# Chunked attention and a gated feed-forward layer on one core: memory values spread in pieces, 1e-9 added by ScalarE, scratch products planned singly, halo rows of two units loaded

## The chip, the cores and the metric

The kernel runs on one core of a Trainium2 chip. The metric is the device time of one execution in microseconds (us). Before the change the median of three runs is 397.0 us (395.86, 397.0, 401.0). The profiled execution, from which all durations below come, took 398.16 us.

## What is computed

Four batches, eight heads, 768 positions, head size 64; the attention looks at a chunk of 32 queries with 16 keys to its left, 8 to its right, and 8 memory keys. Its output, with the heads joined to 512 columns, goes through a gated feed-forward layer.

```python
for c in range(nc):                                   # 24 chunks of 32 queries
    k_ctx, v_ctx = k[:, :, l_start:r_end], v[:, :, l_start:r_end]     # 16 left, 32, 8 right
    k_full = np.concatenate([mem_k, k_ctx], axis=2); v_full = np.concatenate([mem_v, v_ctx], axis=2)
    scores = scale * np.matmul(q_c, k_full.transpose(0, 1, 3, 2))
    a = np.exp(scores - np.max(scores, axis=-1, keepdims=True))
    out[:, :, c_start:c_end] = np.matmul(a / (np.sum(a, axis=-1, keepdims=True) + 1e-09), v_full)
h = np.maximum(x @ w_in, 0.0)                         # x: the attention's output, 512 -> 1024
u, v = h[..., :512], h[..., 512:]
v_n = (v - mean(v)) / np.sqrt(var(v) + 1e-06)
v_s = np.einsum('ts,bsd->btd', w_spatial, v_n) + b_spatial[None, :, None]
return (u * v_s) @ w_out
```

## The kernel before

**Units.** The work on attention is cut into 24 units of 128 queries (four chunks; six units to a batch). For a unit TensorE (PE) makes the scores in a burst of 32 small matmuls (`burst`, line 546, tile `sx`), VectorE (DVE) takes the maximum and subtracts it (lines 635, 639), ScalarE (ACT) takes the exponential (line 654), PE turns the result round with four transposes (line 682, tile `pt`), ACT copies it to `pT` (line 685), and PE multiplies it with the values in a second burst of 32 (line 546, tile `f` for the first three units, `sx` later). DVE scales the product with one over the row sum (`norm`, lines 604 and 609), PE turns it round (line 699, tile `xt`), and ACT and DVE split it into a high and a low part (lines 705 and 709), the input `x` of the feed-forward layer. Here s0, p0 stand for the score burst and the value burst of unit 0, and so on.

**Row sums.** For the first three units (`PSUMS = 3`) PE makes the sums itself: four matmuls of `pT` with a tile of two columns, `halves`, ahead of the value burst; `recip` (lines 620, 622) adds 1e-9 and takes the reciprocal. For later units `den` does it on DVE: a reduction (line 659), the addition of a tile `tiny` that holds 1e-9 (line 660), the reciprocal (line 662).

**Values.** For a chunk, 32 partitions hold its own 32 rows of v, 24 more the halo (the next rows), and the last 8 the memory rows. `vmain` holds three units, `v2` three more. The halo of a unit is either loaded (`load_v` with `halo=True`) or copied on the chip from the next chunk's rows (`shift_v`, line 486, by ACT or GpSimd (POOL), two copies for a unit). The memory rows come by small DMAs on ACT's queue (`load_mem`, `mem_rows`); `spread` and `copy_mem` copy them to all the chunks of `vmain` and `v2` (line 316).

**Weights.** `w_in` comes in eight parts, written here w(c, p): c is one of four slices of 128 rows, p=1 the half that makes v, p=0 the half that makes u. The parts arrive as float64 bits, and `from_f64` turns each into a high and a low float32 part: ACT scales two halves (lines 913, 918), DVE shifts and joins the sign (922, 923), POOL adds (928), ACT casts the high part `win_h` (931), POOL subtracts for the low part `win_l` (935). A feed-forward group for one block of 128 tokens (`ffn_v`, `group`) is four pairs, c = 0 to 3, each of three matmuls with N = 512 (lines 748, 749, 750: high times high, low times high, high times low).

**Order.** `Plan` writes the whole program's order: each operation has an engine, a duration from a table, a rank and its dependencies, and a list scheduler places it; the constants at the top (`FIRST`, `HOT`, `AHEAD`, `SPLIT` and so on) steer it. `FIRST` is the order of the first loads, all on SP's queue, as ("w", c, p, rank, ...), ("qk", group, units, pieces), ("v", unit, units, halo). `AHEAD` is the number of bytes that may be under way on that queue before the next load has to wait for an older one. `HOT` says how many scratch matmuls of a tile `minus` with itself (`heat`, line 306, N = 512, into the spare tile `xt`) stand between the first bursts; nobody reads them. `XLOW` is the number of units whose low part is made by PE and ACT (`rest`, `low_copy`) rather than by DVE. Every engine runs its list strictly in order. In the profile, "issue" is time in which an engine waited for nothing that the profile shows.

Of the kernel before, what the change touches and what calls it, by code (L numbers as in the profile page):

```python
# [8 lines left out]
F32 = mybir.dt.float32  # L9
# [9 lines left out]
CH = 32  # L19
# [14 lines left out]
HOT = (7, 4, 3, 7, 7, 0, 0)  # L34
# [12 lines left out]
SPREAD = {"ACT": 2.6, "POOL": 3.0}  # L47
# [29 lines left out]
class Plan:  # L77
# [36 lines left out]
    def order(self):  # L114
# [19 lines left out]
        while len(out) < len(ops):  # L134
# [29 lines left out]
            if count:  # L164
                k, heat = clock.of(t), 0.5 if count in (128, 256) else 1.0
# [39 lines left out]
def tile_chunked_attention_gmlp(  # L205
# [94 lines left out]

    def heat(n, r=()):
        def go():
            if ("xt", "warm") not in t_:
                alloc("xt", "warm", [P, 512], F32, psum=True)
            for _ in range(n):
                nc.tensor.matmul(t_["xt", "warm"], minus, minus.unsqueeze(1).broadcast_to([P, T, P]), start=True, stop=True, skip_group_check=True)  # L306
# [6 lines left out]
    op("DVE", 0.2, clear, w=["clear"], rank=-1.0)  # L313
# [135 lines left out]
    def load_v(i, units=1, halo=True):  # L449
# [4 lines left out]
        last = (i + units) % GU == 0  # L454
        TS = 2 * NC * D
# [34 lines left out]
    def v_keys(i):  # L490
        mem = [("early", 0, "mem", r, *x) for r in range(2) for x in ((), (1,))] if GU <= i < UB else \
# [5 lines left out]

    def copy_mem():
        for r in range(2):
            rows = slice(r * D + CH, (r + 1) * D)  # L500

            def go(e, rows=rows):
                o = v2[rows, :, 0:NV * UC - 1]
                copy_on(e, o, vmain[rows, :, 0:1].broadcast_to(o.shape))
            op(SPREAD, 0, go, r=[("mv", 0, r, 0)], w=[("early", 0, "mem", r)] +
               [("early", j, "v", r, 3) for j in range(GU, UB)], rank=12.0)
            load(v2[(r + 1) * D - M:(r + 1) * D, :, NV * UC - 1], mem_rows(0, r), w=[("early", 0, "mem", r, 1)],
                 rank=12.0, rows=M, us=0.3)

    def load_mem(b, eng="SP", engines=()):  # L510
        for r in range(2):
            rows = vmain[(r + 1) * D - M:(r + 1) * D]
            if not engines:
                for t in range(T):
# [4 lines left out]
            low = vmain[r * D + CH:(r + 1) * D]  # L519

            def spread(e, low=low):
                o = low[:, :, 1:NV * UC - 1]
                copy_on(e, o, low[:, :, 0:1].broadcast_to(o.shape))
            load(rows[:, :, 0], mem_rows(b, r), r=["clear"], w=[("mv", b, r, 0)], rank=10.0 * UB * b, eng=eng, rows=M,
                 us=0.3)
            load(rows[:, :, NV * UC - 1], mem_rows(b, r), w=[("mv", b, r, 2)], rank=10.0 * UB * b, eng=eng, rows=M, us=0.3)
            op(SPREAD, 0, spread, r=[("mv", b, r, 0)], w=[("mv", b, r, 1)] + [("vm", j, r, 3) for j in range(GU)],
               rank=10.0 * UB * b)
# [15 lines left out]
    def burst(i, rank):  # L544
# [5 lines left out]
        for part in ["sp"] if both else ["s", "p"]:  # L550
# [33 lines left out]
            if i >= 1 and "p" in part:  # L584
# [3 lines left out]
                if part == "p" and i - 1 < PSUMS:  # L588
                    us += 0.6
# [470 lines left out]
```

## Time and profile before

| what | value |
|---|---|
| median of three runs | 397.0 us |
| the profiled execution | 398.16 us |
| its span, first to last instruction | 396.1 us |
| instructions | 11126 |
| PE busy / DVE / ACT / POOL | 383.8 / 195.7 / 165.1 / 110.3 us |
| granted PE clock, mean over the span | 0.983 |
| read from and written to memory | 32.52 and 6.29 MB |

The profile has a page with the busy time of each engine and the span in 40 slices, a chain of waits followed back from the last instruction, groups of instructions with their durations, and tables of stretches of time (busy us of each engine, the granted PE clock, the share and rate of the DMA engines). Times are us from the span's start unless marked ns.

### The profile page before, as it was taken

Reading aid. Unit: us, or ns where it says so; the run is one execution under the profiler, and the core shown is the slowest. Engines: PE = TensorE matmul, PEld = TensorE weight load, DVE = VectorE, ACT = ScalarE, POOL = GpSimd, SP = SyncE. Lnnn points to the kernel's source line nnn. Section 1 sums busy time; section 2 is a strip of 40 time slices with the busy share of each in tenths; the row PEclk is TensorE's granted clock in tenths of the full one; section 3 lists DMA queues with packets and bytes.
Section 4 is the critical chain, followed back from the end, with each engine's and each line's share of the span. In section 5 each row is a group of like instructions: output and inputs, shape, how many; then the busy total and the mean of one; then the engine's idle time right before and its main releaser. Section 6 shows DMA issues by size and latency. Waiting matters only on the chain.

```text
span 396.1 us, 11126 instructions
## 1 busy us (share of the span) xinstructions
PE 383.8 (97%) x4864; PEld 344.3 (87%) x4864; DVE 195.7 (49%) x392; ACT 165.1 (42%) x289; POOL 110.3 (28%) x119
## 2 busy tenths in 40 slices
PE   6797999999999999999999999999999999999996
PEld 4586898999899889889988988889989889899995
DVE  2746987895546447494662315383423233514040
ACT  6686986872524235344323223343221223321212
POOL 6497686285102101010220312010222210104031
PEclk9868999999999999999999999999999999999999
DMA  7999337972165582023746010000001010000202
GB/s 249 263 289 300 120 101 159 280 211 76 43 217 79 133 267 73 2 62 121 164 134 233 1 75 7 0 3 2 2 36 46 26 55 0 0 2 0 81 1 79
DMA packets 29216, 39.53 MB, mean 100 GB/s; under 512 B 5360, under 2 KB 23280, under 8 KB 29168
## 3 DMA queue, kind: packets, MB, share of 16 engines
q1 hardware_dynamic: 28864, 38.73, 32.7%
q8 instruction: 38, 0.62, 0.7%
q10 hardware_dynamic: 304, 0.10, 0.1%
q14 instruction: 10, 0.08, 0.1%
HBM read 32.52 MB, written 6.29 MB: 98 GB/s over the span
## 4 chain that ended last, share of the span: by engine, by line
PE 91%; DMA 7%; issue 1%; POOL 1%; SPq 0%; ACT 0%; POOLq 0%
PE f L748 26%; PE f L749 25%; PE f L750 25%; PE sx L546 8%; DMA vmain<-in_v_dram 3%; PE xt L699 3%; PE pt L682 3%; DMA big<-in_moe_w_in_dram 1%; PE f L546 1%; DMA k<-in_k_dram 1%; DMA vmain<-in_mem_v_dram 1%; PE xt L306 1%; POOL vmain L486 1%; SPq L338 0%; ACT st L890 0%
## 5 line engine op out<-in xcount | busy, mean ns | idle before, releaser
L858 POOL TENSOR_TENSOR st<-st,u 128x384 f32<-128x384 f32 x32 | 33.8, 1057 | 139.3 <-DVE st L854 106.0
L748 PE MATMUL f<-wsp_h,vn 128*128 128x384 f32 x192 | 66.4, 346 | 0.0
L749 PE MATMUL f<-wsp_h,vn 128*128 128x384 f32 x192 | 65.0, 339 | 0.0
L750 PE MATMUL f<-wsp_l,vn 128*128 128x384 f32 x192 | 64.5, 336 | 0.0
L786 POOL TENSOR_TENSOR rstd<-ve,mhalf 128x1 f32<-128x1 f32 x24 | 16.6, 691 | 102.2 <-DVE ve L782 102.2
L748 PE MATMUL f<-x,win_h 128*128 128x384 f32 x128 | 44.7, 350 | 0.0
L861 ACT CAST big<-st 128x384 fp32r<-128x384 f32 x32 | 16.4, 512 | 65.1 <-POOL st L858 65.1
L749 PE MATMUL f<-x,win_l 128*128 128x384 f32 x128 | 43.3, 338 | 0.0
L750 PE MATMUL f<-x,win_h 128*128 128x384 f32 x128 | 43.2, 337 | 0.0
L854 DVE TENSOR_TENSOR st<-f,bias 128x384 f32<-128x384 f32 x32 | 17.8, 556 | 51.3 <-PE f L750 51.3
L748 PE MATMUL f<-win_h,x 128*128 128x512 f32 x96 | 39.7, 413 | 0.0
L748 PE MATMUL f<-wout,big 128*128 128x512 f32 (+1 forms) x100 | 39.0, 390 | 0.0
L749 PE MATMUL f<-wout,big 128*128 128x512 f32 (+1 forms) x100 | 38.3, 383 | 0.0
L750 PE MATMUL f<-wout,big 128*128 128x512 f32 (+1 forms) x100 | 38.2, 382 | 0.0
L750 PE MATMUL f<-win_l,x 128*128 128x512 f32 x96 | 38.1, 397 | 0.0
L749 PE MATMUL f<-win_h,x 128*128 128x512 f32 x96 | 38.0, 396 | 0.0
L748 PEld LDWEIGHTS f<-wsp_h,vn 128*128 128x128 f32 x192 | 36.0, 188 | 1.4
L749 PEld LDWEIGHTS f<-wsp_h,vn 128*128 128x128 f32 x192 | 36.1, 188 | 0.8
L750 PEld LDWEIGHTS f<-wsp_l,vn 128*128 128x128 f32 x192 | 36.1, 188 | 0.0
L778 DVE BATCH_NORM_STATS2 stats<-st 128x6 f32<-128x512 f32 x24 | 16.6, 690 | 31.6 <-ACT st L774 31.6
L865 DVE TENSOR_TENSOR big<-st,big 128x384 fp32r<-128x384 f32 x32 | 20.6, 645 | 21.9 <-ACT big L861 21.6
L890 ACT COPY st<-f 128x512 f32<-128x512 f32 (+1 forms) x25 | 14.2, 571 | 31.3 <-PE f L750 30.9
(85 smaller groups left out, 704.8 us busy)
## 6 DMA issues: line engine op xcount, KB each, us to landing
out_dram<-st SPq DMA_DIRECT2D x23, 256.0 KB
k<-in_k_dram SPq DMA_DIRECT2D x7, 800.0 KB
q<-in_q_dram SPq DMA_DIRECT2D x7, 768.0 KB
vmain<-in_v_dram SPq DMA_DIRECT2D x36, 128.0 KB
big<-in_moe_w_in_dram SPq DMA_DIRECT2D x8, 512.0 KB
vmain<-in_v_dram SPq DMA_DIRECT2D x35, 96.0 KB
big<-in_moe_w_spatial_dram SPq DMA_DIRECT2D x6, 384.0 KB
big<-in_moe_w_out_dram SPq DMA_DIRECT2D x4, 512.0 KB
```

What stands on the lines that cost most here:

```text
L546: nc.tensor.matmul(o, w_, m, start=start, stop=True, skip_group_check=True)
L682: nc.tensor.transpose(a[:, t], p[:, t], ident)
L748: nc.tensor.matmul(o, lh, rh, start=(j == 0), stop=False)
L749: nc.tensor.matmul(o, ll, rh, start=False, stop=False)
L750: nc.tensor.matmul(o, lh, rl, start=False, stop=(j == len(pairs) - 1))
L778: nc.vector.bn_stats(stats, t_["st", s])
L786: nc.gpsimd.tensor_tensor(a, t_["ve", i], mhalf, op=ALU.pow)
L854: nc.vector.tensor_tensor(alloc("st", s_, [P, HT], F32), t_["f", n], bias[:, tok], op=ALU.add)
L858: nc.gpsimd.tensor_tensor(a, a, t_["u", i], op=ALU.mult)
L861: nc.scalar.copy(t_["g", i][:, 0, 0:HT], t_["st", s_])
L865: nc.vector.tensor_tensor(a[:, 1, 0:HT], t_["st", s_], a[:, 0, 0:HT].bitcast(F32), op=ALU.subtract)
L890: nc.scalar.copy(alloc("st", s_, [P, N], F32), t_["f", n])
```

## The change

- **Spreading the memory values.** The eight rows of each head half are loaded once, into chunk 0 of `v2` (two DMAs on ACT's queue, not four there and two on SP's). A helper `spread` then copies that chunk to all of `vmain` and to the rest of `v2`, one copy for each of the four head pairs, over all 128 partitions. The copies into `vmain` now also count as writers of all its rows, so v's first loads come after them. The zeroing (`clear`) is one instruction over 128 partitions.
- **1e-9 by ScalarE.** `den` is cut in three: DVE reduces, ACT adds 1e-9 (`plus`), DVE takes the reciprocal (`over`). `PSUMS` is 0, so no unit has its sums made by PE.
- **Scratch products planned singly.** `heat` enters each scratch matmul as an operation of its own; `HOT` is another list, 37 in all and not 28, one of them in a tile of `f` (`heat_f`).
- **Halo rows loaded.** `FIRST` loads units 4 and 5 with their halo, and `shift_v` is left out for them. The order of the first loads is another, q and k come in two pieces, and `AHEAD` is 1.4 MB, not 2.0.
- `XLOW` is 2, `VACT` 4 and not 6 (units whose normalization is on ACT), `VLOW` may use POOL, and the conversion's shift and sign are two planned operations.

```diff
-AHEAD = 2000000
+AHEAD = 1400000
-FIRST = [("qk", 0, (0, 0), 1), ("mem", 0, "ACT", True), ("qk", 0, (1, 2), 2), ("w", 1, 1, 40.0, 3.0),
+FIRST = [("qk", 0, (0, 0), 2), ("mem", 0, "ACT", True), ("w", 2, 0, 35.0, 27.0, 0),
...
-HOT = (7, 4, 3, 7, 7, 0, 0)
+HOT = (4, 9, 2, 12, 6, 0, 3, 1, 0)
-XLOW = 0
-PSUMS = 3
-VACT = 6
+XLOW = 2
+PSUMS = 0
+VACT = 4
-VLOW = {"DVE": 0.85}
+VLOW = {"DVE": 0.85, "POOL": 1.3}
-SPREAD = {"ACT": 2.6, "POOL": 3.0}
+SPREAD = {"ACT": 0.69, "POOL": 0.78}
...
+    def heat_f(n, r):
+        key_ = ("warm", len(plan.ops))
+        def go():
+            a = alloc("f", key_, [P, 512], F32, psum=True)
+            for _ in range(n):
+                nc.tensor.matmul(a, minus, minus.unsqueeze(1).broadcast_to([P, T, P]), start=True, stop=True,
+                                 skip_group_check=True)
+        if n:
+            op("PE", 0.233 * n, go, r=r, w=[("f", key_)], rank=99.0, tail=0.25, count=2 * n)
...
-            for _ in range(n):
+            for _ in range(1):
                 nc.tensor.matmul(t_["xt", "warm"], minus, minus.unsqueeze(1).broadcast_to([P, T, P]), start=True, stop=True, skip_group_check=True)
-        if n:
-            op("PE", 0.233 * n, go, r=r, w=[("xt", "warm")], rank=99.0, tail=0.25, count=2 * n)
+        for _ in range(n):
+            op("PE", 0.233, go, r=r, w=[("xt", "warm")], rank=99.0, tail=-0.03, count=2)
...
-        for r in range(2):
-            nc.vector.memset(vmain[r * D + CH:(r + 1) * D, :, 0], 0.0)
+        nc.vector.memset(v2[:, :, 0], 0.0)
...
+    def spread(name, dst, c0, keys, rank):
+        for t in range(T):
+            def go(e, t=t):
+                o = dst[:, t, c0:NV * UC]
+                copy_on(e, o, v2[:, t, 0:1].broadcast_to(o.shape))
+            op(SPREAD, 0, go, r=["mv0", "mv1"], w=[(name, t)], rank=rank)
+        op("DVE", 0.0, lambda: None, r=[(name, t) for t in range(T)], w=keys, rank=-1.0)
...
+            load(v2[(r + 1) * D - M:(r + 1) * D, :, 0], mem_rows(b, r), r=["clear"], w=[f"mv{r}"], rank=0.0, eng=eng,
+                 rows=M, us=0.3)
+        if engines:
+            spread("spread", vmain, 0, [("mv", b, r, 1) for r in range(2)] +
+                   [("vm", j, r, x) for j in range(GU) for r in range(2) for x in range(4)], 0.0)
...
             nc.vector.tensor_reduce(d, p3, axis=AX.X, op=ALU.add)
-            nc.vector.tensor_tensor(d, d, tiny, op=ALU.add)
+        def plus():
+            nc.scalar.activation(t_["den", i], t_["den", i], AF.Identity, bias=tiny[:, 0:1])
+        def over():
             rec = t_["rec", i] = small.tile([P, T, 2], F32, tag="rec", name="rec")
-            nc.vector.reciprocal(rec.rearrange("p t r -> p (t r)"), d)
+            nc.vector.reciprocal(rec.rearrange("p t r -> p (t r)"), t_["den", i])
...
-            op("DVE", dve(512) + 0.38, den, r=[("p", i)], w=[("rec", i)], rank=rank + 0.6)
+            op("DVE", dve(512) + 0.02, den, r=[("p", i)], w=[("den", i)], rank=rank + 0.6)
+            op("ACT", 0.21, plus, w=[("den", i)], rank=rank + 0.6)
+            op("DVE", 0.23, over, r=[("den", i)], w=[("rec", i)], rank=rank + 0.6)
...
     for i in range(UB):
-        shift_v(i)
+        if i not in whole_v:
+            shift_v(i)
```

**SP's first loads.** On SP's queue, from the start; `big` is a part of w_in, `v_94` is `v2`. Before:

```order
L338 DMA q<-in_q_dram 128x4x128
L338 DMA k<-in_k_dram 128x4x144
L338 DMA q<-in_q_dram 128x2x256 x2
L338 DMA k<-in_k_dram 128x2x256 x2
L338 DMA big<-in_moe_w_in_dram 128x1024 x4
L338 DMA vmain<-in_v_dram 32x4x768 x2
L338 DMA vmain<-in_v_dram 24x4x64 x2
L338 DMA big<-in_moe_w_in_dram 128x1024
L338 DMA q_297<-in_q_dram 128x4x384
L338 DMA k_158<-in_k_dram 128x4x400
L338 DMA v_94<-in_mem_v_dram 8x4x64 x2
L338 DMA big<-in_moe_w_in_dram 128x1024 x2
```

After:

```order
L348 DMA q<-in_q_dram 128x2x128 x2
L348 DMA k<-in_k_dram 128x2x144 x2
L348 DMA big<-in_moe_w_in_dram 128x1024 x2
L348 DMA q<-in_q_dram 128x2x256 x2
L348 DMA k<-in_k_dram 128x2x256 x2
L348 DMA big<-in_moe_w_in_dram 128x1024 x2
L348 DMA vmain<-in_v_dram 32x4x768 x2
L348 DMA vmain<-in_v_dram 24x4x64 x2
L348 DMA q_300<-in_q_dram 128x2x384 x2
L348 DMA k_153<-in_k_dram 128x2x400 x2
L348 DMA big<-in_moe_w_in_dram 128x1024 x4
```

Four parts of w_in still stand ahead of unit 0's values, in both the last bytes of v end about 4.6 MB into the stream. The fifth part, w(2,1), stood right behind them (before: up to 5.2 MB); now the keys of units 3 to 5 and two other parts, w(0,0) and w(3,0), stand ahead of it, so that it ends at 7.7 MB.

**ACT while unit 0's values come in.** ACT's list from the first copies of halo rows on. Before:

```order
L486 COPY vmain<-vmain 24x4x256 x2
L931 CAST win_h<-st 128x512
L654 ACTIVATE p<-p 128x512
L486 COPY vmain<-vmain 24x4x256
L918 ACTIVATE big<-big 128x512
L931 CAST win_h<-st 128x512
L918 ACTIVATE big<-big 128x512
L685 COPY pT<-pt 128x512
L654 ACTIVATE p<-p 128x512
L931 CAST win_h<-st 128x512
L913 ACTIVATE st<-big 128x512
L316 COPY k_158<-k_158 128x16x24
```

After (the first copy of halo rows and the addition of 1e-9 for unit 1 stand ahead of these):

```order
L498 COPY vmain<-vmain 24x4x256
L952 CAST win_h<-st 128x512
L498 COPY vmain<-vmain 24x4x256
L663 ACTIVATE p<-p 128x512
L701 COPY pT<-pt 128x512
L498 COPY vmain<-vmain 24x4x192
L723 CAST x<-xt 128x4x128
L672 ACTIVATE den<-den,tiny 128x8
L326 COPY k_153<-k_153 128x16x24
L701 COPY pT<-pt 128x512
L737 CAST x<-xt 128x4x128
```

ACT has four copies of halo rows here, not three, and the new instructions `den` and the second `x` (unit 0's low part); fewer conversions stand between them. Behind these rows follow: a cast of a weight, both scalings of w(0,0), x of unit 1, the exponential of unit 3, a scaling of w(3,0), both scalings of w(2,1), unit 1's low part, `pT` of unit 3, `den`, a scaling, x of unit 2, a halo copy of unit 3 and then the cast of w(2,1).

**PE's first feed-forward groups.** With the buffers' numbers: one number of `f` is one block of tokens, in each three rows are one pair c. Before, from the first block's third pair on:

```order
L748 MATMUL f_580<-win_h_107,x_475 128x512
L749 MATMUL f_580<-win_h_107,x_475 128x512
L750 MATMUL f_580<-win_l_108,x_475 128x512
L748 MATMUL f_622<-win_h_107,x_475 128x512
L749 MATMUL f_622<-win_h_107,x_475 128x512
L750 MATMUL f_622<-win_l_108,x_475 128x512
```

After, from the second block's second pair on (`f_582` is the first block, `f_630` the second, `f_653` the third):

```order
L766 MATMUL f_630<-win_h_107,x_473 128x512
L767 MATMUL f_630<-win_h_107,x_473 128x512
L768 MATMUL f_630<-win_l_108,x_473 128x512
L766 MATMUL f_653<-win_h_107,x_473 128x512
L767 MATMUL f_653<-win_h_107,x_473 128x512
L768 MATMUL f_653<-win_l_108,x_473 128x512
L553 MATMUL sx_660<-k1_153,q1_300 32x64 x32
L553 MATMUL sx_660<-v2_94,pT_619 32x64 x32
L766 MATMUL f_582<-win_h_107,x_473 128x512
```

Before, the first block runs through c = 0, 1, 2 with one pair of the second block between, and seven pairs stand ahead of the bursts s4 and p3. Now five pairs stand ahead of them, all with c = 0 and 1, from three blocks; the first pair that needs w(2,1) comes behind p3. Just ahead of all this, where before came p0, its transposes, 7 scratch matmuls, the sums and p1 and the rest up to p2, there now stand p0, a scratch matmul, the transposes of unit 0's output, p1, `pt` of unit 2, unit 0's `rest`, s3, p2, the transposes of unit 1's output, and the first pair.

More of the change, by code (lines that the diff above doesn't have):

```diff
@@ L164, in order @@
             if count:
-                k, heat = clock.of(t), 0.5 if count in (128, 256) else 1.0
+                k, heat = clock.of(t), 0.5 if count in (128, 144, 256) else 1.0
                 us *= k if heat == 1.0 else 1.0 if k == 1.0 else 1.36
@@ L454, in load_v @@
         last = (i + units) % GU == 0
+        if halo:
+            whole_v.update(range(i, i + units))
         TS = 2 * NC * D
@@ L490, in v_keys @@
     def v_keys(i):
-        mem = [("early", 0, "mem", r, *x) for r in range(2) for x in ((), (1,))] if GU <= i < UB else \
+        mem = [("early", 0, "mem", r) for r in range(2)] if GU <= i < UB else \
             [("mv", i // UB, r, s) for r in range(2) for s in range(T)]
@@ L496, in mem_rows @@
         return src(mem_v, (b * H + r) * M * D, [[D, M], [2 * M * D, T], [1, D]])
-    def copy_mem():
[L499 to L508, printed above, removed]
+    def spread(name, dst, c0, keys, rank):
[5 more added lines that the diff above has]
+        op("DVE", 0.0, lambda: None, r=[(name, t) for t in range(T)], w=keys, rank=-1.0)
+    def copy_mem():
+        spread("spread2", v2, 1, [("early", 0, "mem", r) for r in range(2)] +
+               [("early", j, "v", r, x) for j in range(GU, UB) for r in range(2) for x in range(4)], 12.0)
     def load_mem(b, eng="SP", engines=()):
         for r in range(2):
-            rows = vmain[(r + 1) * D - M:(r + 1) * D]
             if not engines:
+                rows = vmain[(r + 1) * D - M:(r + 1) * D]
                 for t in range(T):
@@ L517, in load_mem @@
                 continue
[L519 to L528, printed above, removed]
+            load(v2[(r + 1) * D - M:(r + 1) * D, :, 0], mem_rows(b, r), r=["clear"], w=[f"mv{r}"], rank=0.0, eng=eng,
[3 more added lines that the diff above has]
+                   [("vm", j, r, x) for j in range(GU) for r in range(2) for x in range(4)], 0.0)
     def prep(i, rank):
@@ L588, in burst @@
                 if part == "p" and i - 1 < PSUMS:
-                    us += 0.6
+                    us += 1.05
             if i < 3 and len(hot) > 6:
@@ L592, in burst @@
             op("PE", us, go, r=reads, w=writes, rank=rank, tail=0.25, count=128 * len(part) + (16 if us > 1.3 and part == "p" else 0))
+            if (i, part) == (2, "p") and len(hot) > 8:
+                heat_f(hot[8], [("heat", i, part)])
             if i < 3 and len(hot) > 6 and (i, part) != (2, "p"):
@@ L658, in den @@
             d = small.tile([P, T * 2], F32, tag="den", name="den")
+            t_["den", i] = d
             nc.vector.tensor_reduce(d, p3, axis=AX.X, op=ALU.add)
-            nc.vector.tensor_tensor(d, d, tiny, op=ALU.add)
+        def plus():
+            nc.scalar.activation(t_["den", i], t_["den", i], AF.Identity, bias=tiny[:, 0:1])
+        def over():
             rec = t_["rec", i] = small.tile([P, T, 2], F32, tag="rec", name="rec")
-            nc.vector.reciprocal(rec.rearrange("p t r -> p (t r)"), d)
+            nc.vector.reciprocal(rec.rearrange("p t r -> p (t r)"), t_["den", i])
         sx = ("sx", (i, "sp" if i > SPLIT else "s"), 0)
@@ L688, in flip @@
                 heat(hot[2 + 2 * i], [("turned", i)])
+            if i == 2 and len(hot) > 7:
+                heat_f(hot[7], [("turned", i)])
             op("ACT", act(512), copy, r=[("pt", i)], w=[("pT", i)], rank=rank)
@@ L938, in convert @@
             op("ACT", 0.66, scale_, r=whole + ([] if gate is None else [("p", gate)]), w=[zk], rank=rank)
-            op("DVE", 1.55, shift, r=whole, w=[zk], rank=rank)
+            op("DVE", 0.8, shift, w=[zk], rank=rank)
+            op("DVE", 0.8, sign, r=whole, w=[zk], rank=rank)
             op("ACT", 0.66, rest, r=whole, w=[("big", big, "r")], rank=rank)
```

6 lines of the change are left out of this document (4 added, 2 removed), and 8 rows, old and new, of the table FIRST.

## The prediction

> **What bounds the kernel now.** I read the page's busy times and slices first, then a table of stretches, then the chain of waits where the slices show holes.
>
> ```profile
> span 396.1 us, 11126 instructions
> ...
> PE 383.8 (97%) x4864; PEld 344.3 (87%) x4864; DVE 195.7 (49%) x392; ACT 165.1 (42%) x289; POOL 110.3 (28%) x119
> ...
> PE   6797999999999999999999999999999999999996
> ```
>
> TensorE is the bound, and only the first slices leave anything open. The table says where; its columns are the stretch, its length, the busy us of PE, PEld, DVE, ACT and POOL with the instructions in brackets, the granted clock, the DMA engines' busy share and GB/s:
>
> ```profile
> 0.00:6.25 6.25, 3.29 (x8) 2.16 (x8) 0.81 (x8) 2.80 (x5) 3.17 (x10) 1.00 0.68 205
> 6.25:11.00 4.75, 3.11 (x69) 2.10 (x68) 1.55 (x3) 4.70 (x4) 3.70 (x3) 1.00 0.96 325
> 11.00:18.30 7.30, 5.52 (x78) 4.06 (x78) 6.42 (x8) 3.92 (x7) 3.23 (x3) 0.77 0.96 260
> 18.30:25.00 6.70, 6.31 (x144) 5.53 (x145) 3.29 (x8) 6.62 (x11) 5.31 (x6) 0.58 0.91 281
> 25.00:34.12 9.12, 7.11 (x221) 6.07 (x220) 5.01 (x9) 6.21 (x13) 8.49 (x8) 0.87 0.91 260
> 60.00:120.00 60.00, 59.98 (x963) 54.30 (x963) 40.63 (x77) 33.54 (x61) 25.01 (x23) 1.00 0.55 160
> 135.00:300.00 165.00, 165.00 (x2132) 148.92 (x2131) 77.34 (x163) 57.71 (x106) 22.64 (x30) 1.00 0.24 74
> ```
>
> From 60 us on PE has no idle time (59.98 of 60, 165 of 165). Whatever the change does there to DVE or ACT is covered by a full PE, so the end moves only with the moment at which PE's feed-forward work is under way. That moment is about 34 us; ahead of it PE is half filled with scratch work, the DMA engines run at over 90% and ACT is full from 18 to 25 us (6.62 of 6.70). The chain through this stretch:
>
> ```profile
> 11.04 7.84 DMA vmain<-in_v_dram
> ...
> 20.39 1.04 POOL vmain L486
> 21.48 1.16 PE f L546 x59
> ...
> 23.69 2.83 PE xt L306 x7
> 26.52 1.57 PE f L546 x61
> ...
> 31.25 2.01 issue
> 33.26 0.93 PE f L546 x41
> 34.19 0.72 PE f L748
> ...
> 39.82 0.44 PE xt L699 x4
> ...
> 41.18 0.23 PE f L749
> 41.65 1.69 PE sx L546 x103
> 43.34 0.43 PE f L748
> ```
>
> Unit 0's values land near 20.3 us (the copy of their second half starts at 20.39), p0 runs at 21.48, and then 12.7 us pass to the first feed-forward matmul at 34.19. In them stand 2.83 us of scratch work, two more value bursts with their sums (26.52 is sums and burst together), and 2.01 us for which no wait shows. By 43.34, behind s4 and p3, seven pairs of the feed-forward groups are done. I cost the change up to that point.
>
> **Up to p0: nothing.** The bytes by the table's rates (205 x 6.25, 325 x 4.75 and so on) add up to 1.28, 2.83, 4.72, 6.61 and 8.98 MB at 6.25, 11, 18.3, 25 and 34.12 us. The last row of v ends at about the same byte as before, so it lands near 20.3 us again. The durations around it:
>
> ```profile
> L316 ACT COPY vmain<-vmain 32x2560 f32<-32x2560 f32 x2 | 4.6, 2324 | 0.0
> L316 POOL COPY v<-vmain 32x2816 f32<-32x2816 f32 x2 | 5.1, 2528 | 0.1
> L316 ACT COPY k<-k 128x384 f32<-128x384 f32 x4 | 2.0, 506 | 2.2 <-DMA k<-in_k_dram 2.2
> L486 ACT COPY vmain<-vmain 24x1024 f32<-24x1024 f32 x3 | 3.0, 1042 | 0.0
> L486 ACT COPY v<-v 24x768 f32<-24x768 f32 x1 | 0.8, 829 | 0.0
> ```
>
> A copy's time goes by its elements for one partition, not by its partitions: 384 on 128 partitions take 506 ns, 768 on 24 take 829, 2560 on 32 take 2324. So the eight new copies of 704 or 768 elements cost some 0.8 us each, and four each on ACT and POOL are 3.2 us for 4.6 and 5.1. That frees 1.4 and 1.9 us, at 5 to 10 us, when both wait for loads again soon after; two of them now stand ahead of the first copy of keys, which puts s0 about 1 us later. Both are hidden behind the v load, which p0 needs in either order. Bounds: 1 us either way. Were v to land early, s0's lateness would still have 10 us to spare. PE's sums for three units go too, three groups of four matmuls, but on a PE that waits: they are worth only what the next part finds.
>
> **From v's landing to p3.** Now PE has less of its own, and ACT's list decides. Its durations:
>
> ```profile
> L931 ACT CAST win_h<-st 128x512 fp32r<-128x512 f32 x8 | 4.8, 614 | 0.0
> L654 ACT ACTIVATE p<-p 128x512 f32<-128x512 f32 x6 | 3.8, 631 | 2.9 <-DVE p L639 2.8
> L685 ACT COPY pT<-pt 128x512 f32<-128x512 f32 x6 | 3.5, 582 | 0.0
> L705 ACT CAST x<-xt 128x512 fp32r<-128x512 f32 x5 | 2.9, 583 | 2.6 <-PE xt L699 2.6
> L913 ACT ACTIVATE st<-big 128x512 f32<-128x512 f32 x8 | 5.4, 675 | 3.4 <-DMA big<-in_moe_w_in_dram 3.4
> L918 ACT ACTIVATE big<-big 128x512 uint32<-128x512 uint32 x8 | 5.5, 683 | 0.0
> L296 ACT ACTIVATE warm<-mhalf 128x1 f32<-128x1 f32 x1 | 0.2, 203 | 0.0
> L660 DVE TENSOR_TENSOR den<-den,tiny 128x8 f32<-128x8 f32 x21 | 6.2, 293 | 0.7
> L935 POOL TENSOR_TENSOR win_l<-st,win_h 128x512 fp32r<-128x512 f32 x8 | 10.2, 1287 | 0.4 <-ACT win_h L931 0.4
> ```
>
> The addition of 1e-9 on ACT is in no row; the small activation of 203 ns bounds it from below and DVE's own 128x8 addition, 293 ns, from above; I take 0.2, and a wait of DVE for it falls on no chain here. From 20.39 ACT works off: copy 1.04, cast 0.61, copy 1.04, exponential 0.63, pT of unit 1 0.58, copy 0.83, x of unit 0 0.58, the addition 0.2, keys 0.51, pT of unit 2 0.58. That is 6.6 us: 27.0. PE meets each of these in time (p0 at 21.5, unit 0's transposes near 24, p1 after 24.3), so p2 starts at 27.0, and with 0.93 for it and 0.44 for the transposes the first feed-forward matmul comes at **28.4, not 34.2**.
>
> That lead is not kept. ACT goes on with x low 0.58, a cast 0.61, two scalings 1.36, x of unit 1 0.58, the exponential of unit 3 0.63 and a scaling 0.68: 31.46. Only now comes w(2,1). It ends at 7.7 MB, by the rates at 29.3 us, so it has been there for 2.1 us. Its scalings take to 32.8, unit 1's low part to 33.4. PE's transposes of unit 2 need the `xt` that this low part still reads: PE has done two pairs and waits to 33.4, transposes (0.44), makes the second block's two pairs (six matmuls at 0.23, 1.4 us) to 35.2, waits for unit 2's x (ACT 35.4, DVE's low part 36.1), makes one pair, and s4 and p3 (1.69) end at 38.5. Here five pairs are done, before it was seven at 43.34; the two missing take 1.4. So at equal work PE stands at 39.9 for 43.3: **3.4 us early**. The cast of w(2,1) ends at 37.1 and POOL's low part at 38.4, in time for the pair behind p3.
>
> Two costs come off. One is the clock:
>
> ```profile
> 29.61:33.03 3.42, 1.64 (x61) 1.36 (x46) 2.56 (x7) 2.74 (x6) 2.88 (x4) 1.00 1.00 236
> 33.03:36.45 3.42, 3.19 (x49) 2.63 (x49) 1.95 (x5) 0.63 (x1) 1.27 (x2) 0.50 0.92 303
> ```
>
> After a stretch of 3.4 us in which PE was busy for 1.64, the next 3.4 us ran at half clock. The changed list has such a hole at 30 to 33.4 again, with transposes and a few matmuls in it. Bounds: 0, or half of 3.4 us, 1.7; I take 0.9, since ACT holds PE for part of that time anyway. The Trainium skill, "TensorE: Matmul & The Clock Gate", Part 1 (the HAM clock gate), has the gate close after an idle window of about 3.4 us; the row shows a half-idle window to do it. By the page nothing would come off here. The other cost is the 2.01 us of "issue" in p2's burst. Nothing moved says it goes; it can come back at the same burst, where 1.1 of it would be hidden by ACT (x of unit 1 is not due before 29.56). Bounds 0 and 0.9; I take 0.5.
>
> **Sum.** 3.4 - 0.9 - 0.5 = 2.0 us off the profiled execution's 398.16 (span 396.1 and 2.06 around it): 396.2. That execution lies 1.16 above the median of the runs, 397.0, so the median becomes **395.0 us**. Per unit later on, 21 additions go from DVE to ACT: PE covers them. The loads of halos in place of copies, 0.13 MB more, lie behind w(1,0), where the stream is not what is waited for.
>
> **Rivals.**
>
> 1. *POOL takes the lead back.* From 31.4 on POOL has the additions and low parts of the last four weights and a halo copy:
>
> ```profile
> L928 POOL TENSOR_TENSOR st<-st,big 128x512 uint32<-128x512 uint32 x8 | 11.0, 1381 | 7.5 <-DVE st L923 6.3 <-ACT big L918 1.2
> ```
>
> Four of 1.38, four of 1.29 and 1.04 are 11.7 us, to 43.1 without any wait, while PE has seven pairs and a value unit, some 6 us, from 38.5 to 44.5 before it needs them. With 1.5 us of waits for ACT in between, 0 to 2 us are lost: about **397.0**, no change. For it: POOL was busy 8.49 of 9.12 us before 34; against: before, it was later still.
>
> 2. *The stream is slower, and the kernel with it.* Less may be under way (1.4 MB), and the first loads come in more and smaller pieces. v's landing moves the whole ACT list one for one. 4.6 MB by 20.3 us is 225 GB/s; 10% less puts v at 22.5, 20% less at 25.4. So a loss of 9% eats the 2.0 us, and a loss of 20% gives 395.0 + 5.1 = **400.1**, slower than before. For it: the slowest stretch (260) holds v itself. Against: loads of 262 KB already moved in the row at 325 GB/s, and 1.4 MB at that rate is 4.3 us of work under way. The Trainium skill, "DMA: Bandwidth & Descriptors", section Bandwidth, asks for loads of 1 MiB or more for 75% of the peak; by it the halved loads speak for this rival. The trace's 325 with loads of a quarter of that size does not agree.
>
> 3. *Nothing comes off*: PE's idle time spreads over two windows, the clock stays up, and the 2.01 us do not return. Then all 3.4 are kept: **393.6**. That the gate's windows lie differently in each run makes it possible in some.
>
> A fourth, that the new order reaches a later stage that is short of loads, has little behind it: PE was at 14.92 of 15 us where the second batch's values arrive.
>
> ```profile
> 120.00:135.00 15.00, 14.92 (x299) 13.24 (x286) 9.37 (x18) 4.71 (x9) 3.04 (x3) 1.00 0.70 137
> ```
>
> **How the numbers follow.** Chances: the forecast 0.45, POOL's tail 0.20, the slower stream 0.20, all kept 0.15. Two per cent, about what a measurement of this kernel can tell from no change, is 7.9 us: below 389.1 or above 404.9. Below 389.1 more would have to go than ACT's list allows (the first pair at 28.4 and no stall after is 5.8); I give it 0.06. Above 404.9 the stream would have to lose a third; 0.04. The range reaches from the full gain and 3 us of what I overlook, 390.5, to the slower stream at 20%, 400.5. The three runs before spread over 5.1 us, so single runs say little here.
>
> **What would show it.** Right: the first L766 matmul near 28 to 30.5 us and the end of p3 near 38.5 to 41; a hole of PE before unit 2's transposes whose releaser is ACT; DVE's waits for the addition of 1e-9 on no chain; no PE idle time after 60 us. Wrong: v's copies start later than 21.5 (rival 2); PE waits on POOL's L956 between 43 and 60 (rival 1); first pairs early and yet no time gained, or PE holes in a later batch, for which I have no mechanism.

## The result, and the profile after

The changed kernel takes 400.14 us (median of 20 runs, 397.79 to 402.51); the kernel before, measured beside it, 397.92 us (20 runs, 395.86 to 402.9). The ratio is 1.005, with a 95% interval of 1.0026 to 1.0074: 0.5% slower, some 2.0 us by this ratio, where 2 us faster was forecast. The profiled execution took 401.82 us, 1.7 above its median; the one of before lies 0.2 above the median of its 20 runs, so the two traces stand further apart (3.7 us) than the kernels do. Some executions of a kernel are over 1.5% slower than its fastest: the ratios here and below leave them out, the medians do not.

The page of the changed kernel, and its stretches of time (columns as in the prediction):

```profile
span 400.0 us, 11124 instructions
...
PE 381.3 (95%) x4851; PEld 339.5 (85%) x4851; DVE 193.4 (48%) x368; ACT 167.6 (42%) x315; POOL 103.9 (26%) x117
...
q8 instruction: 38, 0.62, 0.7%
```

```profile
25.00:34.12 9.12, 6.91 (x218) 5.33 (x217) 5.71 (x13) 7.50 (x15) 4.32 (x8) 1.00 0.73 232
34.12:43.34 9.22, 7.32 (x145) 4.97 (x146) 5.36 (x8) 6.95 (x13) 5.47 (x5) 0.81 0.74 223
43.34:60.00 16.66, 14.16 (x196) 12.03 (x196) 13.01 (x27) 11.61 (x23) 11.61 (x11) 1.00 0.75 214
135.00:300.00 165.00, 163.58 (x2242) 146.96 (x2241) 78.83 (x156) 60.84 (x118) 21.74 (x30) 1.00 0.27 78
```

The stretches from 34.12 to 60 us in the trace of before:

```profile
34.12:43.34 9.22, 9.22 (x165) 7.45 (x162) 7.84 (x17) 7.21 (x11) 5.61 (x7) 0.87 0.84 293
43.34:60.00 16.66, 16.33 (x331) 14.71 (x332) 14.47 (x30) 15.22 (x27) 12.87 (x12) 1.00 0.31 96
```

PE works 2.5 us less than before, and the span is 3.9 longer. The two places where PE is idle and hardly was before are 34 to 60 us (7.32 + 14.16 of 25.88, so 4.4 idle, before 0.3) and 135 to 300 us (1.4 idle, before 0). Ahead of 34 us the change did much of what it was expected to. Rows of PE's list from 23 to 56 us, with the waits in square brackets:

```profile
23.83 0.86 PE L553 MATMUL f<-vmain,pT 64*32 64x64 f32 x64
...
30.47 0.45 PE L553 MATMUL f<-vmain,pT 64*32 64x64 f32 x29 [0.93 <-issue]
...
31.26 0.48 PE L766 MATMUL f<-win_h,x 128*128 128x512 f32 x1
...
35.74 0.66 PE L717 MATMUL xt<-ident,xs 128*128 128x128 f32 x4 [2.18 <-ACT x L737]
...
40.74 1.21 PE L553 MATMUL sx<-v,pT 64*32 64x64 f32 x64
...
43.84 0.39 PE L766 MATMUL f<-win_h,x 128*128 128x512 f32 x1
...
46.11 0.63 PE L717 MATMUL xt<-ident,xs 128*128 128x128 f32 x4 [1.40 <-DVE xs L613]
...
55.63 0.63 PE L717 MATMUL xt<-ident,xs 128*128 128x128 f32 x4 [1.10 <-DVE xs L613]
```

The first feed-forward matmul comes at 31.26, before it was 34.12, and the hole ahead of unit 2's transposes (2.18, released by ACT's low part) is the one that the prediction named. Behind p3 stand two holes that it did not name (1.40 and 1.10 us), both until DVE's scaling `xs`. DVE's rows ahead of the two holes, then POOL's:

```profile
42.03 1.02 DVE L940 TENSOR_SCALAR st<-st 128x512 uint32<-128x512 uint32 x1 [2.72 <-ACT st L931]
43.08 1.69 DVE L944 SCALAR_TENSOR_TENSOR st<-big,st 128x512 uint32<-128x512 uint32 x1
44.69 0.68 DVE L644 TENSOR_REDUCE mx<-sx 128x8 f32<-128x512 f32 x1
45.29 0.67 DVE L613 TENSOR_TENSOR xs<-sx,rec 128x512 f32<-128x512 f32 x1
...
52.43 1.53 DVE L812 SCALAR_TENSOR_TENSOR shift<-mvar,rstd 128x1 f32<-128x1 f32 x1
```

```profile
41.48 1.28 POOL L956 TENSOR_TENSOR win_l<-st,win_h 128x512 fp32r<-128x512 f32 x1 [0.41 <-ACT win_h L952]
42.73 1.49 POOL L949 TENSOR_TENSOR st<-st,big 128x512 uint32<-128x512 uint32 x1
...
52.10 1.84 POOL L992 TENSOR_TENSOR wsp_l<-big,wsp_h 128x768 fp32r<-128x768 f32 x1
```

L812 works on one element for each partition, and takes 1.53 us: it ends 0.02 us after POOL's L992. L944 takes 1.69, and POOL's L949 fills 1.14 of them. The same instructions beside an idle POOL take 146 ns (one case) and 682 ns (seven cases). L613, one operand of which lies in PSUM (the memory of PE's results), takes its usual 0.67. The reading (theory E below) is that a DVE instruction that takes two operands from SBUF (the memory of all other tiles) stands still until the POOL instruction that started ahead of it ends. Ahead of the first hole DVE also waited 2.72 us for ACT; which of the two made that hole these rows alone do not tell.

The third place is the last group's keys. The chain of waits of the changed kernel there, and the loads' issues of the kernel before:

```profile
207.89 0.29 SPq L348
...
210.69 5.95 DMA q<-in_q_dram
216.72 4.94 DMA k<-in_k_dram
221.69 0.52 ACT k L326
...
222.30 1.61 PE sx L553 x100
```

```profile
204.50 0.39 SPq L338 DMA_DIRECT2D q<-in_q_dram  x1
205.09 0.39 SPq L338 DMA_DIRECT2D k<-in_k_dram  x1
```

Queries of 0.79 MB and keys of 0.82 MB are together more than the 1.4 MB that may now be under way. So the keys are issued when the queries have landed, 6.0 us behind them, where they went 0.6 us behind them before, and PE waits 1.26 us at 221 us.

### The profile page after: what moved, and what is told of

It is laid out like the page before. It is cut to its first block, busy times and chain, and to the rows that moved or that the text cites. A ratio compares the mean times of both kernels' runs of the same rounds, so it can differ in the third digit from the quotient of the medians.

```text
span 400.0 us, 11124 instructions
## 1 busy us (share of the span) xinstructions
PE 381.3 (95%) x4851; PEld 339.5 (85%) x4851; DVE 193.4 (48%) x368; ACT 167.6 (42%) x315; POOL 103.9 (26%) x117
## 4 chain that ended last, share of the span: by engine, by line
PE 82%; DMA 13%; SPq 2%; DVE 1%; ACT 1%; issue 0%; ACTq 0%
PE f L766 24%; PE f L767 23%; PE f L768 23%; PE sx L553 7%; DMA k<-in_k_dram 5%; DMA q<-in_q_dram 5%; DMA big<-in_moe_w_in_dram 4%; PE xt L717 2%; PE pt L698 2%; SPq L348 2%; DVE shift L812 0%; DVE stats L796 0%; ACT k L326 0%; DVE mx L644 0%; DVE xs L613 0%
## 5 line engine op out<-in xcount | busy, mean ns | idle before, releaser
L883 DVE TENSOR_TENSOR big<-st,big 128x384 fp32r<-128x384 f32 x32 | 22.0, 686 | 21.2 <-ACT big L879 20.8
L553 PEld LDWEIGHTS sx<-k,q 64*32 64x32 f32 x1536 | 17.1, 108 | 13.5 <-issue 7.5
```

The source lines that it names most:

```text
L553: nc.tensor.matmul(o, w_, m, start=start, stop=True, skip_group_check=True)
L883: nc.vector.tensor_tensor(a[:, 1, 0:HT], t_["st", s_], a[:, 0, 0:HT].bitcast(F32), op=ALU.subtract)
```

## The experiments

All ratios are to the kernel before, run on the same chip; the changed kernel has 1.0050 (1.0026 to 1.0074). An effect of 1 us is 0.0025, about half the width of an interval, so the trace of each is read beside its time. "Lists as they are" means that every engine's order of instructions is that of the changed kernel.

| kernel | median us | before us | ratio, 95% interval |
|---|---|---|---|
| a_wait20 | 401.34 | 398.9 | 1.0044 (1.0013 to 1.0075) |
| a_wait28 | 401.85 | 398.9 | 1.0062 (1.0030 to 1.0094) |
| b_wait14 | 412.3 | 398.9 | 1.0341 (1.0292 to 1.0390) |
| a_plusdve | 399.16 | 398.9 | 1.0026 (0.9995 to 1.0058) |
| a_mix44 | 399.27 | 398.72 | 1.0021 (0.9991 to 1.0052) |
| a_mix24 | 400.1 | 398.72 | 1.0040 (1.0009 to 1.0070) |
| a_mix22 | 399.45 | 398.72 | 1.0010 (0.9977 to 1.0044) |
| a_ahead20 | 411.21 | 398.72 | 1.0326 (1.0273 to 1.0379) |
| a_shift1 | 398.92 | 398.79 | 1.0012 (0.9987 to 1.0038) |
| a_order | 399.92 | 398.79 | 1.0020 (0.9994 to 1.0045) |
| a_page | 407.01 | 398.79 | none given |
| a_sum | 398.19 | 398.79 | 0.9964 (0.9934 to 0.9995) |
| a_sum2 | 396.67 | 398.76 | 0.9964 (0.9935 to 0.9993) |
| a_act | 400.35 | 398.76 | 1.0047 (1.0014 to 1.0080) |
| a_sum3 | 398.02 | 398.76 | 0.9992 (0.9965 to 1.0019) |

### Bytes under way, lists as they are

The first theory was the second rival of the prediction: the 1.4 MB limit holds the loads back (A). Against it stood that the lists' order costs the time (B), and the addition of 1e-9 on ACT (C). The limit that the order is planned with stays; a second one, `WAIT`, sets the waits that are issued.

```diff
-AHEAD = 1400000
+AHEAD = 1400000; WAIT = 2000000
...
-            if before:
+            if hold:
```

`hold` is the newest older load that must have landed with `WAIT`, as `before` is with `AHEAD`.

> The changed kernel with every engine's list as it is; only the loads' wait is set at 2.0 MB under way, not 1.4. Theory A (the 1.4 MB rule holds the loads back): v's first load is issued near 11 to 12 us (15.92 in the changed kernel), p0 starts before 23 us (23.83), PE's idle time of 4.4 us from 34 to 60 us falls under 2, the keys of the last group are issued right behind its queries and PE's 1.3 us of idle time at 221 us is gone; time 396 to 398 us. Theory B (the new order of ACT's and DVE's lists costs the time, whatever the loads do): the holes stay, 399.5 to 400.5 us. Theory C (the addition of 1e-9 on ACT delays 1/sum): as B.

> The changed kernel with the same lists, the wait at 2.8 MB. Theory A: as with 2.0 MB or up to 0.7 us less, if the 2.0 MB still bind somewhere; if later loads then share the engines with the urgent ones, v lands later than with 2.0 MB and the time is up to 1 us more. Theories B and C: 399.5 to 400.5 us.

> The kernel before with every engine's list as it was; only the loads' wait is set at 1.4 MB, not 2.0. Theory A: v's first load is issued 3 to 5 us later than 11.04, PE's dense work starts later, and the queries and keys of the last group come one behind the other; time 400 to 402 us, 2 to 4 more than before. Theories B and C: within 0.5 us of before, 397.5 to 398.5.

Theory A as it was put fell. With 2.0 MB the stream was again as fast as before (269 GB/s up to 34.12 us, before 263, changed kernel 236) and the hole at 221 us shrank to 0.3, and yet nothing came off. PE's rows with a wait from 18 to 36 us in a_wait20 show why:

```profile
21.94 0.79 PE L317 MATMUL xt<-minus 128*128 128x512 f32 x1 [2.85 <-issue]
29.34 0.63 PE L717 MATMUL xt<-ident,xs 128*128 128x128 f32 x4 [0.50 <-DVE xs L618]
35.08 0.67 PE L553 MATMUL f<-vmain,pT 64*32 64x64 f32 x29 [2.13 <-issue]
```

Two stalls for which no wait shows, 5.0 us in all, where the changed kernel has one of 0.93; with 2.8 MB they are 2.69 and 2.46. Behind the first, nine scratch matmuls took 4.19 us, not 2.32, and p0 started only at 27.35. That more bytes under way make the stalls longer fits these two runs, but not all (below). The kernel before, with its own lists, is another matter: its limit alone, at 1.4 MB, costs 3.4% (five of its six runs took 411.0 to 415.2 us, one 1266 for a reason that stays open). Its waits of PE from 34 us on:

```profile
PE sx L546 <- ACT k L316: 7.7, 4, 2.3
```

Four groups' keys wait for their queries there, 7.7 us; the changed kernel's lists, planned with 1.4 MB, leave one such hole. The limit is thus worth what the order around it makes of it. A new order made with 2.0 MB shows the same from the other side:

```diff
-AHEAD = 1400000
+AHEAD = 2000000
```

> The changed kernel planned anew with 2.0 MB, so that planner and waits agree and all lists are other ones. Theory D: the hole at 221 us is absent, stalls without a known wait of 2 to 5 us stand in the first 35 us as with 2.0 MB under the old lists; 399 to 401.5 us. Theory B (the lists decide): up to 3 us either way, 397 to 403.

411.21 us is outside every expectation: stalls of 2.4 and 2.0 us without a known wait, and 9.6 us of waits for ACT and DVE from 34 us on. These other lists cost 3.3%, about as much as the limit alone cost the kernel before; why the planner's lists are worse here stays open.

### From where on the limit binds

Theory D: not the first loads, but two places with late ones. `WAIT` becomes a function of the load's number.

```diff
-AHEAD = 1400000
+AHEAD = 1400000; WAIT = lambda i: 2800000 if i >= 44 else AHEAD
```

> The changed kernel, lists as they are; from the 45th load on (all behind the first loads, so from the values of the second batch on) the loads' wait is at 2.8 MB, ahead of it 1.4. Theory D (the changed kernel loses at two places by late loads: some 3 us from 34 to 56 us, and 1.3 us at 221 us, where the keys of the last group, 0.82 MB, wait for its queries, 0.79 MB): PE's idle time at 221 us goes, that from 34 to 60 us stays; 1.0 to 1.4 us less than the changed kernel, 398.7 to 399.1 where that has 400.1. Theory B (the lists alone): no change.

> The changed kernel, lists as they are; the wait is at 2.8 MB from the 25th load on (the values of units 3 to 5 and all behind them), ahead of it 1.4. Theory D: the hole at 221 us goes, ACT's wait for the values of unit 3 (2.25 us at 37.4 us) falls below 1 and with it PE's holes at 44.7 and 54.4 us; p2's burst keeps its 0.9 us without a known wait, since no more bytes are under way at 29 us than before; 2.5 to 3.5 us less than the changed kernel, 396.6 to 397.6. Theory B: no change.

> The changed kernel, lists as they are; the wait is at 2.0 MB from the 23rd load on (w(2,1) and all behind it), ahead of it 1.4. Theory D: w(2,1) is issued 3 to 4 us earlier, PE's hole at 33.6 us shrinks from 2.2 to about 1.4; but if bytes under way hold up the instructions' own loads, p2's burst loses 1.5 to 2.5 us where it lost 0.9: within 0.7 us of the run with 2.8 MB from the 25th load on. Theory B: no change.

(a_mix24 has 24 for 44, a_mix22 has 22 and 2.0 MB.) a_mix44 did as theory D said for the hole at 221 us (1.26 to 0.54), and 1.0021 agrees with 1 us. In a_mix24 ACT's wait of 2.2 us for unit 3's values is gone from its waits, and still PE has 1.6 us of holes until DVE's `xs` (2.5 in the changed kernel), and the time does not fall by the 2.5 to 3.5 us expected. DVE shows no wait there from 36.3 us on and still comes to `xs` when it did in the changed kernel (45.29):

```profile
43.05 1.67 DVE L944 SCALAR_TENSOR_TENSOR st<-big,st 128x512 uint32<-128x512 uint32 x1
...
45.25 0.67 DVE L613 TENSOR_TENSOR xs<-sx,rec 128x512 f32<-128x512 f32 x1
```

So the late loads alone do not make those holes, and that part of theory D fell. The stall in p2's burst answers two expectations otherwise than they were put: in a_mix24 it is 2.03 us, though up to it the limit is the 1.4 MB of the changed kernel (0.9 was expected), and in a_mix22, where w(2,1) goes out at about 26.7 us and not at 28.98, it is 0.81. The bytes under way do not by themselves set its length. By its centre a_mix22 is 1.6 us under the changed kernel, with intervals that overlap; a_mix44's share of that, the hole at 221 us, is 1.2. What an earlier w(2,1) is worth besides these runs cannot tell.

### The addition of 1e-9

```diff
-            nc.scalar.activation(t_["den", i], t_["den", i], AF.Identity, bias=tiny[:, 0:1])
+            nc.vector.tensor_tensor(t_["den", i], t_["den", i], tiny, op=ALU.add)
```

> The changed kernel with the addition of 1e-9 on DVE at the same place of the program and everything else as it is. Theory C (ACT's additions, 24 of 0.30 us, and DVE's wait for them cost the time): 398 to 399 us. Theories A and B: within 0.5 us of the changed kernel, 399.6 to 400.6.

1.0026: 0.9 us under the changed kernel by its centre, within the intervals of both. The addition's place decides nothing that these runs can show.

### DVE beside POOL

Theory E is the reading of the DVE and POOL rows in the section on the result. Two edits test it, one for each hole. The first gives L812 a form with one tensor in SBUF and two scalars:

```diff
-            nc.vector.scalar_tensor_tensor(a, t_["mvar", i][:, 0:1], -1.0, t_["rstd", i], op0=ALU.mult, op1=ALU.mult)
+            nc.vector.tensor_scalar(a, t_["mvar", i][:, 0:1], t_["rstd", i], -1.0, op0=ALU.mult, op1=ALU.mult)
```

> The changed kernel with one DVE instruction in another form: the product of mean and 1/deviation (128x1) as an operation with one tensor and two scalars, not with two tensors. Theory E (a DVE instruction that reads two tensors in SBUF waits until POOL's running instruction ends; in the changed kernel this one took 146 ns alone and 1158 ns on the average of the three beside POOL): it takes 0.2 us everywhere, and PE's hole near 54 us (1.10 us) goes; up to 1 us less than the changed kernel. Theory D (late loads alone make the holes): the hole stays, no change.

The second moves three planned operations, numbers 68, 69 and 71 (shift, sign and POOL's addition of w(1,0)), behind number 219, unit 4's difference:

```diff
-        for n in self.order():
+        for n in moved(self.order()):
```

> The changed kernel with two DVE instructions (shift and sign of w(1,0)) and the POOL addition behind them moved behind unit 4's maximum, unit 3's scaling and unit 4's difference. In the changed kernel they stood ahead, and ran 1.02 and 1.69 us for 0.42 and 0.68. Theory E: unit 3's transposes no longer wait (PE's hole of 1.40 us at 44.7 us goes), nothing new waits for w(1,0); up to 1.4 us less. Theory D: the hole stays, since it hangs on the late loads of ACT's list.

The group of L812 in the changed kernel, then in a_shift1 (busy us and mean ns behind the bar):

```profile
L812 DVE SCALAR_TENSOR_TENSOR shift<-mvar,rstd 128x1 f32<-128x1 f32 x4 | 3.6, 905 | 0.1
```

```profile
L812 DVE TENSOR_SCALAR shift<-mvar,rstd 128x1 f32<-128x1 f32 x4 | 0.8, 202 | 0.0
```

A mean of 905 ns (two of 0.15 us, 1.53 and 1.79) became 202 with POOL's work as it was. PE's waits from 34 us on in the changed kernel (us in all, times, longest), then the row for `xs` in a_shift1 and in a_order:

```profile
PE xt L717 <- DVE xs L613: 2.5, 2, 1.4
PE xt L717 <- ACT x L737: 2.2, 1, 2.2
PE sx L553 <- ACT k L326: 1.3, 1, 1.3
PE f L768 <- POOL win_l L956: 0.2, 1, 0.2
```

```profile
PE xt L717 <- DVE xs L613: 1.4, 1, 1.4
```

```profile
PE xt L717 <- DVE xs L613: 1.8, 1, 1.8
```

Each edit takes one of the two holes away, as theory E said, and leaves the other (in a_order at 53.9 us, 1.8 long that time). a_shift1 changes nothing but the form of L812, and so shows the cause of the second hole. a_order also takes DVE's wait for ACT out of the way of `xs`, so for the first hole it shows that DVE's list was the cause; that POOL lengthened this list rests on the durations (1.02 and 1.69 us for 0.42 and 0.68) and on a_mix24. The ratios fall by 0.0038 and 0.0030, each with intervals that overlap; the sum below goes further. The Trainium skill, "SBUF — State Buffer", section Who interferes with whom, states the rule: a VectorE instruction with two inputs in SBUF contends with a GpSimd instruction that reads SBUF, and the second to start is blocked until the first ends. This trace agrees: of L944's twelve, the four that started behind a POOL instruction took 1.20 to 1.69 us, and one that started 0.1 us ahead of POOL's copy took 0.68, the copy 1.46 for 1.03. L940, which has one input, was lengthened too: 0.91 to 1.51 us in the five that started behind a POOL instruction, 0.37 to 0.43 in the others.

### PE's stall in p2's burst

Theory F: the "issue" stall is PE waiting for its next block of instructions. Fifteen scratch matmuls of 512 columns become sixty of 128, which puts 45 pairs of instructions more ahead of p0.

```diff
-            for _ in range(1):
+            done[0] += 1; parts = T if 10 < done[0] <= 25 else 1
```

> The changed kernel with 15 scratch matmuls of 512 columns as 60 of 128, so that 45 more pairs of PE instructions stand ahead of p0 and every block of 256 PE instructions ends 45 pairs earlier in the work. Theory F (the stall without a known wait in p2's burst, 0.8 to 2.0 us in five runs, is PE waiting for its next block of instructions, which the bursts use up faster than it comes): the stall leaves its place 39 pairs into p2's burst, for a place 6 pairs before the end of s3's burst, and is shorter by up to 1 us; 0 to 1 us less. Otherwise the stall stays in p2's burst at the same pair.

The bursts s3 and p2 of a_page, where the changed kernel stalled at 35 of p2's 64 matmuls:

```profile
28.43 0.78 PE L553 MATMUL sx<-k,q 64*32 64x64 f32 x55
29.92 0.32 PE L553 MATMUL sx<-k,q 64*32 64x64 f32 x9 [0.71 <-issue]
30.07 0.93 PE L553 MATMUL f<-vmain,pT 64*32 64x64 f32 x64
```

The stall has moved forward by 44 matmuls (9 of s3 and 35 of p2), as far as 45 pairs put it. So it hangs on the count of instructions, and on nothing that the matmul needs. The DMA records of the traces bear theory F out: in 15 profiles with 18 such stalls ahead of 36 us, each stall ended 1.2 to 1.6 us after a 16 KB packet of the "instruction" queue had landed (in the changed kernel the packet landed at 28.98 us, PE went on at 30.47). The packet took 0.9 to 1.3 us each time; what varied was when it started, and why is not shown. The profile page's "instruction" queue has 38 packets, 0.62 MB, 16 KB each; 4851 matmuls with as many weight loads are 9702 instructions, 37.9 times 256. A block of 256 is 128 pairs, and s3 and p2 use up 128 in 1.7 us. The time of a_page (400.1 to 410.2 us) says nothing on this: 48 of its narrow scratch matmuls stood right ahead of s2 and took 5.58 us, where the changed kernel's twelve wide ones took 4.60. The Trainium skill, "Runtime: NRT & Kernel Launch", section Instruction fetch mechanics, has the same blocks of 16 KiB and 256 instructions, and the cost of crossing one mostly hidden. This trace agrees for most of the 38 blocks: the changed kernel has only two waits of this kind on PE, 0.93 and 0.2 us. In the dense bursts it was not hidden: the 18 stalls are 0.6 to 2.9 us long.

### ACT's list, and the sums

```diff
+MOVE = {201: [59, 62, 60, 61], 67: [100]}
```

Both scalings of w(2,1) and DVE's two steps go behind number 201, unit 3's addition of 1e-9; the halo copy of unit 3 goes behind number 67, a scaling.

> The changed kernel with ACT's list in another order at two places and everything else as it is: the two scalings of w(2,1) behind unit 1's low part (and the two DVE instructions that follow them, whose order stays), and the halo copy of unit 3, which waits for its load, behind the cast of w(2,1) and a scaling. Theory D (ACT, held by late loads in its list, holds PE): PE's hole at 33.6 us, 2.2 to 3.0 us in four runs, falls under 1 us, and 1 to 1.5 us come off. If the pairs behind it then lack w(2,1), the hole only moves on, and the time stays within 0.5 us of the changed kernel.

The hole at 33.6 us fell from 2.18 to 0.24, and came back in three others. PE's waits in a_act from 34 us on:

```profile
PE xt L717 <- DVE xs L613: 1.5, 1, 1.5
PE sx L553 <- ACT v L498: 1.3, 1, 1.3
PE f L766 <- ACT x L723: 0.8, 1, 0.8
```

Another order inside ACT's list gained nothing (1.0047); that ACT was behind as a whole there is a reading of these waits, not shown by an edit.

a_sum has a_shift1, a_order, a_page and the limit of a_mix44 in one kernel, a_sum2 the same without a_page, a_sum3 is a_sum2 with a_act.

> All three edits together, and the loads' wait at 2.8 MB from the 45th load on. If the terms add up (0.8 to 1.1 from the keys of the last group, 0.6 to 1 from the product's form, 0.7 to 1.4 from DVE's order, 0 to 1 from the blocks of instructions), 2 to 4 us less than the changed kernel: 396 to 398 where that has 400.1 and the kernel before 397.9. If something else sets the end (the load of v, the clock), within 1 us of the changed kernel.

> The changed kernel with the three edits that left the scratch work alone: the product in another form, DVE's order, and the loads' wait at 2.8 MB from the 45th load on. If these terms add up as they did with the split scratch matmuls (0.9964 of the kernel before), 396.5 to 398 us where the kernel before has 398.8, without the runs of 404 to 407 us; the holes of PE at 44, 54 and 221 us are gone. If the gain there came from the split scratch work, 399 us or more.

> Both together. If the terms add up, 395 to 397 us where the kernel before has 398.8, which is the time that the prediction gave the changed kernel (2 us less than before). If the lead made in the first 40 us cannot be kept, as the run with the three edits alone.

a_sum2 is 0.36% faster than the kernel before, and the spread of its runs (396.15 to 397.98) is the smallest of all. PE's stretches in it:

```profile
34.12:43.34 9.22, 6.56 (x146) 5.23 (x145) 4.56 (x8) 7.57 (x14) 6.26 (x6) 0.81 0.93 283
43.34:60.00 16.66, 16.55 (x209) 14.29 (x207) 12.48 (x29) 13.61 (x26) 10.69 (x9) 1.00 0.69 193
135.00:300.00 165.00, 164.90 (x2145) 148.73 (x2131) 78.42 (x155) 61.04 (x118) 21.78 (x30) 1.00 0.25 78
```

The idle time from 43 to 60 us went from 2.50 to 0.11, that from 135 to 300 us from 1.42 to 0.10. Singly the three edits lower the ratio by 0.0029, 0.0038 and 0.0030, together by 0.0086, some 3.4 us, and here the intervals of the changed kernel and of a_sum2 are apart. a_sum, whose profile is of an execution of 404.8 us and is not read here, has the same ratio as a_sum2. a_sum3 is slower than a_sum2 by its centre, 0.9992, with intervals that overlap.

## Why the prediction was wrong, step by step

- **"Up to p0: nothing." This term failed, by 2.4 us in the profiled execution; its bounds were 1 us either way.** The copies were sized right (0.83 and 0.77 us for 0.8) and stayed hidden. But p0 ran at 23.83 us, not 21.48. One part is v: SP's next load waited for it until 21.94. (The 20.3 of the prediction is only an upper bound: the copy at 20.39 stood behind another copy on POOL and waited for no load.) Another part is scratch work, which the term did not have:

```profile
15.57 4.60 PE L317 MATMUL xt<-minus 128*128 128x512 f32 x12
...
21.58 2.32 PE L317 MATMUL xt<-minus 128*128 128x512 f32 x9
```

```profile
21.96 1.04 ACT L498 COPY vmain<-vmain 24x1024 f32<-24x1024 f32 x1
```

  ACT's copy (the last row) ended at 23.00, and PE was at its scratch matmuls until p0; twelve of them had taken 4.60 us, at a granted clock of 0.57 from 16 to 20 us, where six other kernels with the same list took 3.0 and found p0 waiting for that copy. In nine other kernels with PE's list and the limit unchanged up to there, the main part of p0 started at 22.2 to 25.0 us, late in all. The second rival has this place and about this size: it priced a stream slower by 10% at 2.2 us, and the stream was 10% slower (236 for 263 GB/s up to 34.12 us). Its other case, 400.1 us, meets the measured 400.14 by luck: it stood on v at 25.4 us. That 2.0 MB would give the speed back and p0 come no earlier was not foreseen.
- **From v's landing to p3: held.** With the two costs in it (0.5 ahead of the first feed-forward matmul, 0.9 behind) the prediction has 7.4 us from p0 to that matmul and 11.0 from there to p3's end; 7.4 and 10.6 were measured. The hole until ACT's low part came where it was named. But p3 ended at 41.9, and the eighth pair, which started at 43.34 before, starts at 43.84: 0.5 us late where 2.0 early was forecast, and p0's 2.4 are the reason.
- **The two costs.** The granted clock was 0.81 from 34 to 43 us (before 0.87), so a stretch at half clock came, as charged (0.51 from 36.8 to 40.0 us). The stall that shows no wait came back with 0.93 us where 0.9 was the bound and 0.5 the choice.
- **"... the end moves only with the moment at which PE's feed-forward work is under way." This is the step that failed most.** The prediction read in the trace of before that PE has no idle time from 60 us on, took it that a full PE covers whatever the change does to DVE or ACT, and costed the change up to 43.34 us only; from there to 60 it left a loss to the first rival. But PE is full in that trace with the lists of that kernel. From 43.34 to 60 us PE is idle for 2.50 us in the changed kernel, before for 0.33: all of the 2.50 is the two holes until DVE's `xs`, behind instructions that wait for POOL (the 1.9 idle from 34.12 to 43.34 are mostly the forecast hole until ACT, 1.6, and 0.2 until a low part). The first rival had the place, the conversions behind p3, and the wrong way to PE: POOL's work reached it through DVE, and not through late low parts (0.2 us). A row of the prediction held the sign: L660 has a mean of 293 ns over 21, and in the trace of before it takes 167 alone and up to 1392 beside POOL.
- **"PE holes in a later batch, for which I have no mechanism."** The mechanism stood in the change: 0.79 + 0.82 MB is more than 1.4 MB, once for every later group. One hole of 1.26 us came of it, behind 60 us, where the full PE was to cover the change. The stretch from 60 us to the end, before and after:

```profile
60.00:400.00 340.00, 332.91 (x3858) 302.23 (x3856) 156.29 (x311) 118.39 (x218) 67.88 (x74) 1.00 0.26 77
```

```profile
60.00:400.00 340.00, 335.68 (x3996) 304.75 (x3994) 155.71 (x296) 123.91 (x239) 67.91 (x75) 1.00 0.26 77
```

At 60 us PE had 2.8 us of work more ahead of it than before, and up to the end of its span (396.1 and 400.0 us) it is idle 1.1 us longer: that is the 3.9 us of span. The 2.8 are the 0.5 at the eighth pair and the 2.2 of longer idle time up to 60 us, to within 0.1.

The three edits that answer to the last two points give back 3.4 us, by the centres of the ratios, of the 4.0 between forecast and result. They did not bring the forecast lead about: in a_sum2 the main part of p0 still starts at 23.25 us. No experiment brought p0 back to 21.5, so what its delay costs in the end, and what makes v late, stay open.

## What to carry to other kernels

That the engine which bounds the kernel is full in a trace shows that the present order feeds it, not that it covers what another order does: take each in-order list of the change past the point where the lead is made. Look for instructions whose mean hides two durations, and see what runs beside the long ones; a form with one operand in SBUF instead of two can be worth more than a move to another engine. Where a limit on bytes under way is lowered, compare it with the largest pair of loads that one stage needs together.

## What the hardware showed that was not expected

- A 128x1 instruction on DVE took up to 1.79 us beside POOL and 0.15 alone; a POOL copy that started 0.1 us behind a DVE instruction was lengthened too, from 1.03 to 1.46 us.
- PE stalled in dense bursts until 1.2 to 1.6 us after a 16 KB packet of its instructions had landed. The stall in p2's burst was 0.6 to 1.7 us in eight kernels with 1.4 MB under way, 2.13 and 2.46 with 2.0 and 2.8 MB; but it was 2.03 in a_mix24, at 1.4 MB, and 0.81 in a_mix22, at up to 2.0, so that data loads lengthen it is not shown.
- 128x8 on ACT took 303 ns, more than either bound of the forecast (203 and 293).
